# A radix-47 by 64 DFT through DRAM in place of dense DFT matmuls, issued between the MLP steps of the batch ahead

## Chip, cores, metric

One core of one Trainium2 chip. The metric is device time of one execution in microseconds (us); lower is better. A ratio is the mean time of one kernel's fast runs over the mean of the other's fast runs of the same rounds, so it is not quite the ratio of the medians that are quoted beside it. "Batch period" below means the distance between the same point of two successive batches, as a mean of the middle six of one trace: the first matmul of the forward DFT in the kernel before, the first hidden matmul in all other runs.

Engines: PE is TensorE (matmuls), PEld its weight loads, DVE is VectorE, ACT is ScalarE, POOL is GpSimd, SP is SyncE (here only an issuer of DMAs). A "column" is one column of a matmul's moving operand. PSUM holds the tiles that matmuls write here, SBUF those that they read; an "evacuation" is a ScalarE or VectorE copy from PSUM to SBUF. The "pitch" is the time from the start of one matmul to the start of the next, and the "head" is all that comes before the first hidden matmul.

## The reference

A global filter along the sequence, by FFT, followed by an MLP with a "snake" activation:

```
x: [8, 3008, 256]   filt_r, filt_i: [1505, 256]
X = rfft(x, axis=1);  y = irfft(X * (filt_r + 1j*filt_i), n=3008, axis=1)
h = y.reshape(24064, 256) @ w_in           # w_in  [256, 2048]
s = sin(alpha * h)
out = (h + s*s / alpha) @ w_out            # w_out [2048, 256]
```

Both kernels use `out = y @ (w_in @ w_out) + (s*s) @ (w_out / alpha)`. So the MLP has a hidden matmul (y to 2048 features), a Sin on ScalarE, a square on VectorE and a projection.

## The kernel before

The sequence is split into even and odd positions (`r`). Each half is transformed by one dense matmul against cosine and sine tables, combined with the filter on VectorE, and transformed back by another dense matmul. Everything of one batch runs in this order; only the scheduling of independent engines overlaps.

```python
for b in range(B):
    ...                                       # load x, two tiles of 128 x 12 x 256, f16
    for i in range(6):                        # forward DFT
        for p in range(2):                    # cos, sin
            for k in range(12):
                nc.tensor.matmul(out=psA[:, p, :], lhsT=lhs, rhs=xr_tiles[0][0:nrow, k, :], ...)  # 256 columns
                nc.tensor.matmul(out=psB[:, p, :], lhsT=lhs, rhs=xr_tiles[1][0:nrow, k, :], ...)
        nc.scalar.copy(out=asb, in_=psA)
        nc.scalar.copy(out=bsb, in_=psB)
        ...                                   # 28 VectorE operations on 128 x 256: filter and twiddles -> Z
    for r in range(2):
        for cb in range(2):                   # inverse DFT
            for (m0, n) in tok_chunks:        # 512, 512, 480
                for i in range(6):
                    for p in range(2):
                        nc.tensor.matmul(out=psy[:, 0:n], lhsT=Z[r][p][:, i, ...],
                                         rhs=e_t[:, p, i, m0:m0 + n], ...)
                nc.scalar.copy(out=ysb[:, cb, m0:m0 + n], in_=psy[:, 0:n])
        for (m0, n) in tok_chunks:            # MLP
            for jb in range(16):
                ...                           # 2 hidden matmuls of n columns
                nc.scalar.activation(out=vt[:, jb, 0:n], in_=psh[:, 0:n], func=AFT.Sin,
                                     scale=alpha_t[:, jb:jb + 1])
                nc.vector.tensor_tensor(...)  # square
            for t in range(nblk):             # projection: 18 matmuls of 256 columns per 128 tokens
                ...                           # one PSUM buffer; VectorE copy; store to DRAM
```

Of the kernel before, what the change touches and what calls it, by code (L numbers as in the profile page):

```python
# [12 lines left out]
ALU = mybir.AluOpType  # L14


@with_exitstack
def kernel(
# [11 lines left out]
    B, S, C = 8, 3008, 256  # L30
    N = S
    M = S // 2
    NQ = 753
    NQP = 768
    DFF = 2048

    mm = np.arange(M, dtype=np.float64)
    qq = np.arange(NQP, dtype=np.float64)
    qmask = (qq < NQ).astype(np.float64)
    ang = 2.0 * np.pi * np.outer(mm, qq) / M  # L40
    dt_cos = np.cos(ang) * qmask[None, :]
    dt_sin = -np.sin(ang) * qmask[None, :]
    dt_full = np.concatenate([dt_cos, dt_sin], axis=1)
    dt_host = np.zeros((128, 12, 2 * NQP), dtype=np.float16)
    for k in range(12):
        nrow = min(128, M - 128 * k)
        dt_host[:nrow, k, :] = dt_full[128 * k:128 * k + nrow].astype(np.float16)
    e_host = np.zeros((128, 2, 6, M), dtype=np.float16)
    angqm = 2.0 * np.pi * np.outer(qq, mm) / M
    ecos = (np.cos(angqm) * qmask[:, None]).astype(np.float16)  # L50
    esin = (-np.sin(angqm) * qmask[:, None]).astype(np.float16)
    for i in range(6):
        e_host[:, 0, i, :] = ecos[128 * i:128 * (i + 1)]
        e_host[:, 1, i, :] = esin[128 * i:128 * (i + 1)]
    qv = qq.reshape(6, 128).T
    wq = np.where((qv == 0) | (qv == M // 2), 1.0, 2.0) / N
    wq = wq * (qv < NQ)
    wc = wq * np.cos(2 * np.pi * qv / N)
    ws = wq * np.sin(2 * np.pi * qv / N)
    ident_np = np.eye(128, dtype=np.float32)  # L60
    revj_np = np.eye(128, dtype=np.float32)[::-1].copy()

    dt_dram = nc.inline_tensor(dt_host, name="dt_tbl")
    e_dram = nc.inline_tensor(e_host, name="e_tbl")
    w3_dram = nc.inline_tensor(
        np.stack([wq, wc, ws], axis=1).astype(np.float32), name="w3_tbl"
    )
    ident_dram = nc.inline_tensor(ident_np, name="ident")
    revj_dram = nc.inline_tensor(revj_np, name="revj")

    out3 = out.rearrange("(b s) c -> b s c", b=B)

    cpool = ctx.enter_context(tc.tile_pool(name="consts", bufs=1))
    dt_t = cpool.tile([128, 12, 2 * NQP], FP16)
    e_t = cpool.tile([128, 2, 6, M], FP16)
    nc.sync.dma_start(out=dt_t, in_=dt_dram.ap())
    nc.sync.dma_start(out=e_t, in_=e_dram.ap())
    w3_t = cpool.tile([128, 3, 6], FP32)
    nc.sync.dma_start(out=w3_t, in_=w3_dram.ap())
    P0re = cpool.tile([128, 6, C], FP16)  # L80
    P0im = cpool.tile([128, 6, C], FP16)
    Q0re = cpool.tile([128, 6, C], FP16)
    Q0im = cpool.tile([128, 6, C], FP16)
    P1re = cpool.tile([128, 6, C], FP16)
    P1im = cpool.tile([128, 6, C], FP16)
    w_in16 = cpool.tile([128, 2, DFF], FP16)
    nc.gpsimd.dma_start(out=w_in16, in_=moe_w_in.rearrange("(a p) j -> p a j", p=128))
    w_out2 = cpool.tile([128, 16, C], FP16)
    m_t = cpool.tile([128, 2, C], FP16)
    alpha_t = cpool.tile([128, 16], FP32)  # L90
    nc.sync.dma_start(
        out=alpha_t, in_=moe_alpha.rearrange("(a p) -> p a", p=128)
    )
    recip_a = cpool.tile([128, 16], FP32)
    nc.vector.reciprocal(out=recip_a, in_=alpha_t)  # L95

    with tc.tile_pool(name="init", bufs=1) as ipool:
        ident_t = ipool.tile([128, 128], FP32)
        nc.sync.dma_start(out=ident_t, in_=ident_dram.ap())  # L99
        w_in32 = ipool.tile([128, 2, DFF], FP32)  # L100
        nc.sync.dma_start(
            out=w_in32, in_=moe_w_in.rearrange("(a p) j -> p a j", p=128)
        )
        w_out32 = ipool.tile([128, 16, C], FP32)
        nc.sync.dma_start(
            out=w_out32, in_=moe_w_out.rearrange("(b p) c -> p b c", p=128)
        )
        w_out16 = ipool.tile([128, 16, C], FP16)
        w_inT = ipool.tile([128, 16, C], FP16)
        with tc.tile_pool(name="initps", bufs=2, space=bass.MemoryType.PSUM) as ipps:  # L110
            for jb in range(16):
                nc.vector.tensor_scalar(
                    out=w_out2[:, jb, :], in0=w_out32[:, jb, :],
                    scalar1=recip_a[:, jb:jb + 1], scalar2=None, op0=ALU.mult,
                )
                nc.gpsimd.tensor_copy(out=w_out16[:, jb, :], in_=w_out32[:, jb, :])
                for cb in range(2):
                    pst = ipps.tile([128, 128], FP32, tag="pst")
                    nc.tensor.transpose(  # L119
                        out=pst, in_=w_in32[:, cb, jb * 128:(jb + 1) * 128],  # L120
                        identity=ident_t,
                    )
                    nc.vector.tensor_copy(  # L123
                        out=w_inT[:, jb, cb * 128:cb * 128 + 128], in_=pst
                    )
            for cb in range(2):
                psm = ipps.tile([128, 512], FP32, tag="psm")
                for jb in range(16):
                    nc.tensor.matmul(  # L129
                        out=psm[:, 0:C],  # L130
                        lhsT=w_inT[:, jb, cb * 128:cb * 128 + 128],
                        rhs=w_out16[:, jb, :],
                        start=(jb == 0), stop=(jb == 15),
                    )
                nc.vector.tensor_copy(out=m_t[:, cb, :], in_=psm[:, 0:C])
        fr_f = ipool.tile([128, 6, C], FP32)
        fi_f = ipool.tile([128, 6, C], FP32)
        fr_b = ipool.tile([128, 6, C], FP32)
        fi_b = ipool.tile([128, 6, C], FP32)
        nc.sync.dma_start(  # L140
            out=fr_f, in_=filt_r[0:768].rearrange("(i p) c -> p i c", p=128)
        )
        nc.sync.dma_start(
            out=fi_f, in_=filt_i[0:768].rearrange("(i p) c -> p i c", p=128)
        )
        revj_t = ipool.tile([128, 128], FP32)
        nc.sync.dma_start(out=revj_t, in_=revj_dram.ap())
        tfwd = ipool.tile([128, 2, C], FP32)
        with tc.tile_pool(name="revps", bufs=2, space=bass.MemoryType.PSUM) as rpps:
            for i in range(6):  # L150
                row0 = 1377 - 128 * i
                nc.sync.dma_start(out=tfwd[:, 0, :], in_=filt_r[row0:row0 + 128, :])
                nc.sync.dma_start(out=tfwd[:, 1, :], in_=filt_i[row0:row0 + 128, :])
                psrev = rpps.tile([128, 512], FP32, tag="psrev")
                nc.tensor.matmul(out=psrev[:, 0:2 * C], lhsT=revj_t, rhs=tfwd[:, :, :])  # L155
                nc.vector.tensor_copy(out=fr_b[:, i, :], in_=psrev[:, 0:C])
                nc.vector.tensor_copy(out=fi_b[:, i, :], in_=psrev[:, C:2 * C])
        gre = ipool.tile([128, C], FP32)
        gim = ipool.tile([128, C], FP32)
        hre = ipool.tile([128, C], FP32)  # L160
        him = ipool.tile([128, C], FP32)
        ta = ipool.tile([128, C], FP32)
        tb = ipool.tile([128, C], FP32)
        tc_ = ipool.tile([128, C], FP32)
        td = ipool.tile([128, C], FP32)
        for i in range(6):
            wv = w3_t[:, 0, i:i + 1]
            wcv = w3_t[:, 1, i:i + 1]
            wsv = w3_t[:, 2, i:i + 1]
            nc.vector.tensor_tensor(out=gre, in0=fr_f[:, i, :], in1=fr_b[:, i, :], op=ALU.add)  # L170
            nc.vector.tensor_tensor(out=hre, in0=fr_f[:, i, :], in1=fr_b[:, i, :], op=ALU.subtract)
            nc.vector.tensor_tensor(out=gim, in0=fi_f[:, i, :], in1=fi_b[:, i, :], op=ALU.subtract)
            nc.vector.tensor_tensor(out=him, in0=fi_f[:, i, :], in1=fi_b[:, i, :], op=ALU.add)
            if i == 0:
                nc.vector.memset(gim[0:1, :], 0.0)
                nc.vector.memset(him[0:1, :], 0.0)
            nc.vector.tensor_scalar(out=P0re[:, i, :], in0=gre, scalar1=wv, scalar2=None, op0=ALU.mult)
# [19 lines left out]

    tok_chunks = [(0, 512), (512, 512), (1024, 480)]

    for b in range(B):  # L200
        xr_tiles = []
        for r in range(2):
            xt = xpool.tile([128, 12, C], FP16, name=f"x_{b}_{r}", tag=f"x{r}")
# [139 lines left out]
```

## Time and profile before

| | before |
|---|---|
| median of 3 runs | 1392.51 us (1391.48 to 1394.24) |
| first hidden matmul | 156.0 us |
| batch period | 159.4 us |
| TensorE busy in one period | 155.13 us |
| VectorE, ScalarE busy in one period | 88.66, 69.96 us |

The page of the kernel before: busy time per engine, then busy tenths in 40 equal slices of the span ("9" is 90% or more), the granted TensorE clock and the DMA share in the same slices, and the chain of waits that ended last as shares by engine.

```profile
span 1388.4 us, 21372 instructions
PE 1277.2 (92%) x8524; PEld 818.9 (59%) x8524; DVE 752.6 (54%) x2453; ACT 562.1 (40%) x962; POOL 33.2 (2%) x53
...
PE   0629899989999999999999899998999999998998
...
PEclk9859999999999999999999999999999999999999
DMA  9442310030000310121000300103100000000101
...
PE 72%; DVE 21%; SPq 2%; DMA 2%; issue 1%; ACT 1%; POOL 0%; ACTq 0%; DVEq 0%; POOLq 0%
```

TensorE is the limit from the fifth slice on. The head is the exception: the first hidden matmul starts at 156 us.

The table of busy time by stretch of the kernel before: a stretch in us, its length, busy us of each engine with the number of instructions, granted clock, DMA share, GB/s. The stretches are the head and one steady batch.

```profile
core 0: us, PE busy (x) PEld busy (x) DVE busy (x) ACT busy (x) POOL busy (x), PEclk, DMA share, GB/s
0.00:156.00 156.00, 76.86 (x436) 47.66 (x437) 82.14 (x317) 10.91 (x18) 16.88 (x33) 0.85 0.56 145
...
258.10:417.50 159.40, 155.13 (x1059) 100.57 (x1058) 88.66 (x289) 69.96 (x121) 3.27 (x4) 1.00 0.14 30
```

"Busy" must not be read as "at its peak": a matmul's busy span includes time in which the next one already streams. The timeline gives the pitch. Its columns are start, length, engine, line, operation, operands, shapes, count, and in brackets the idle time before it with what ended it. Kernel before, inverse DFT:

```profile
301.29 0.39 PE L261 MATMUL psy_0_0_0_2641<-e_t,z_0_1_2133 128*128 128x512 f16 x1 [2.28 <-DVE z_0_1_2133 L253]
301.51 0.38 PE L261 MATMUL psy_0_0_512_2655<-e_t,z_0_0_2132 128*128 128x512 f16 x1
301.73 0.38 PE L261 MATMUL psy_0_0_512_2655<-e_t,z_0_1_2133 128*128 128x512 f16 x1
```

Each matmul is listed as 0.38 us long, but they start 0.216 us apart: 512 columns in 0.216 us, 2.37 columns per ns. A batch has 352.8 thousand columns, hence 149 of its 159.4 us. The remaining 10 us are waits and paced stretches, such as the 2.28 us on VectorE here.

### The profile page before, as it was taken

The page shows a single profiled execution, that of the slowest core. Times are in us where ns is not written, and L with a number is a line of the kernel's source. Part 1 is how long each engine was busy: PE and PEld are TensorE (multiplying, and loading weights), DVE is VectorE, ACT ScalarE, POOL GpSimd, SP SyncE. Part 2 cuts the span into 40 slices and gives each one's busy share as a digit, 9 for nine tenths or more (in the row PEclk, how much of TensorE's full clock was granted, in tenths as well). Part 3 has the DMA queues.
Part 4 walks back from the last instruction along what each step waited for, and adds up shares of the span by engine and source line. Part 5 has one row for each costly group of instructions (what it writes and reads, how often), then busy time and mean ns, then how long its engine had stood idle before and what let it go on. Part 6 is the DMA issues. An engine that isn't in the chain of part 4 may idle for free.

```text
span 1388.4 us, 21372 instructions
## 1 busy us (share of the span) xinstructions
PE 1277.2 (92%) x8524; PEld 818.9 (59%) x8524; DVE 752.6 (54%) x2453; ACT 562.1 (40%) x962; POOL 33.2 (2%) x53
## 2 busy tenths in 40 slices
PE   0629899989999999999999899998999999998998
PEld 0208465765568465775658565684657655684655
DVE  0757644495256753495355753486444952566534
ACT  0002546316361454416362264414463164613544
POOL 0110000000000000000000000000000000000000
PEclk9859999999999999999999999999999999999999
DMA  9442310030000310121000300103100000000101
GB/s 335 165 66 40 52 38 16 31 45 24 23 31 16 45 35 22 35 35 27 30 24 23 46 31 15 39 10 51 38 16 30 2 23 23 31 15 1 35 19 38
DMA packets 60500, 56.21 MB, mean 40 GB/s; under 512 B 6128, under 2 KB 59632, under 8 KB 59888
## 3 DMA queue, kind: packets, MB, share of 16 engines
q1 hardware_dynamic: 35552, 41.48, 8.6%
q0 software_dynamic: 24848, 13.37, 7.1%
q8 instruction: 66, 1.08, 0.3%
q14 instruction: 34, 0.28, 0.1%
HBM read 43.57 MB, written 24.64 MB: 49 GB/s over the span
## 4 chain that ended last, share of the span: by engine, by line
PE 72%; DVE 21%; SPq 2%; DMA 2%; issue 1%; ACT 1%; POOL 0%; ACTq 0%; DVEq 0%; POOLq 0%
SPq L99 2%; DMA tfwd<-in_filt_i_dram 1%; PE psrev L155 1%; DMA x_1_431<-in_x_dram 1%; PE pst L119 1%; DMA w_in_83<-in_moe_w_in_dram 1%; ACT v_1_1024_13843 L279 0%; PE psm L129 0%; PE psB_0_439 L229 0%; PE psy_0_0_1024_12857 L261 0%; DVE w_inT L123 0%; PE psA_0_7230 L226 0%; PE psA_0_12324 L226 0%; PE psA_0_8928 L226 0%; PE psA_0_3834 L226 0%
## 5 line engine op out<-in xcount | busy, mean ns | idle before, releaser
L273 PEld LDWEIGHTS <-w_in_70 128*128 128x128 f16 x1536 | 149.3, 97 | 101.0 <-issue 19.9
L226 PEld LDWEIGHTS <-dt_t 128*128 128x128 f16 (+1 forms) x1152 | 113.0, 98 | 35.9 <-issue 21.6
L229 PEld LDWEIGHTS <-dt_t 128*128 128x128 f16 (+1 forms) x1152 | 113.5, 99 | 15.7 <-issue 1.4
L119 PE MATMUL pst<-ident_t,w_in_83 128*128 128x128 f32 x32 | 10.6, 402 | 39.7 <-DMA w_in_83<-in_moe_w_in_dram 37.9
L234 ACT ACT_TABLE_LOAD x1 | 1.3, 1283 | 110.1 <-PE psA_0_438 L226 110.1
L119 PEld LDWEIGHTS pst<-ident_t,w_in_83 128*128 128x128 f32 x32 | 5.3, 168 | 44.9 <-issue 37.8
L226 PE MATMUL psA_0_438<-x_0_428,dt_t 128*128 128x256 f16 (+1 forms) x24 | 6.5, 379 | 20.1 <-DMA x_0_428<-in_x_dram 20.1
L155 PE MATMUL psrev<-tfwd,revj_t 128*128 128x512 f32 x12 | 10.4, 963 | 14.2 <-DMA tfwd<-in_filt_i_dram 13.6
L95 DVE RECIPROCAL recip_a<-alpha_t 128x16 f32<-128x16 f32 x1 | 0.3, 255 | 31.2 <-DMA alpha_t<-in_moe_alpha_dram 31.2
L283 DVE TENSOR_TENSOR v_1_0_6713<-v_1_0_6713 128x512 f16<-128x512 f16 x16 | 6.8, 426 | 15.7 <-ACT v_1_0_6713 L279 15.7
L283 DVE TENSOR_TENSOR v_1_0_1619<-v_1_0_1619 128x512 f16<-128x512 f16 x16 | 6.8, 425 | 15.7 <-ACT v_1_0_1619 L279 15.7
L283 DVE TENSOR_TENSOR v_1_0_10109<-v_1_0_10109 128x512 f16<-128x512 f16 x16 | 6.8, 425 | 15.7 <-ACT v_1_0_10109 L279 15.7
L283 DVE TENSOR_TENSOR v_1_0_13505<-v_1_0_13505 128x512 f16<-128x512 f16 x16 | 6.8, 425 | 15.7 <-ACT v_1_0_13505 L279 15.7
L283 DVE TENSOR_TENSOR v_1_0_3317<-v_1_0_3317 128x512 f16<-128x512 f16 x16 | 6.8, 425 | 15.7 <-ACT v_1_0_3317 L279 15.7
L283 DVE TENSOR_TENSOR v_1_0_5015<-v_1_0_5015 128x512 f16<-128x512 f16 x16 | 6.8, 425 | 15.7 <-ACT v_1_0_5015 L279 15.7
L283 DVE TENSOR_TENSOR v_1_0_8411<-v_1_0_8411 128x512 f16<-128x512 f16 x16 | 6.8, 425 | 15.7 <-ACT v_1_0_8411 L279 15.7
L283 DVE TENSOR_TENSOR v_1_0_11807<-v_1_0_11807 128x512 f16<-128x512 f16 x16 | 6.8, 425 | 15.7 <-ACT v_1_0_11807 L279 15.7
L155 PEld LDWEIGHTS psrev<-tfwd,revj_t 128*128 128x128 f32 x12 | 2.6, 269 | 20.6 <-issue 16.1
L123 DVE CAST w_inT<-pst 128x128 f16<-128x128 f32 x32 | 8.4, 290 | 10.2 <-PE pst L119 10.1
L283 DVE TENSOR_TENSOR v_0_0_12913<-v_0_0_12913 128x512 f16<-128x512 f16 x16 | 6.8, 426 | 10.7 <-ACT v_0_0_12913 L279 10.6
L283 DVE TENSOR_TENSOR v_0_0_1027<-v_0_0_1027 128x512 f16<-128x512 f16 x16 | 6.8, 426 | 10.3 <-ACT v_0_0_1027 L279 10.1
L283 DVE TENSOR_TENSOR v_0_0_9517<-v_0_0_9517 128x512 f16<-128x512 f16 x16 | 6.8, 425 | 8.9 <-ACT v_0_0_9517 L279 8.9
(3457 smaller groups left out, 3845.5 us busy)
## 6 DMA issues: line engine op xcount, KB each, us to landing
dt_t<-dt_tbl SPq DMA_DIRECT2D x1, 4608.0 KB, 15.6
e_t<-e_tbl SPq DMA_DIRECT2D x1, 4512.0 KB, 28.7
w_in_83<-in_moe_w_in_dram SPq DMA_DIRECT2D x1, 2048.0 KB, 7.6
w_out_85<-in_moe_w_out_dram SPq DMA_DIRECT2D x1, 2048.0 KB, 13.1
w_in_70<-in_moe_w_in_dram POOLq DMA_DIRECT2D x1, 1024.0 KB, 29.0
fr_f<-in_filt_r_dram SPq DMA_DIRECT2D x1, 768.0 KB, 14.9
fi_f<-in_filt_i_dram SPq DMA_DIRECT2D x1, 768.0 KB, 10.6
tfwd<-in_filt_r_dram SPq DMA_DIRECT2D x6, 128.0 KB, 2.0
```

The lines of the kernel that those rows point to most:

```text
L95: nc.vector.reciprocal(out=recip_a, in_=alpha_t)
L99: nc.sync.dma_start(out=ident_t, in_=ident_dram.ap())
L119: nc.tensor.transpose(out=pst, in_=w_in32[:, cb, jb * 128:(jb + 1) * 128], identity=ident_t,)
L123: nc.vector.tensor_copy(out=w_inT[:, jb, cb * 128:cb * 128 + 128], in_=pst)
L155: nc.tensor.matmul(out=psrev[:, 0:2 * C], lhsT=revj_t, rhs=tfwd[:, :, :])
L226: nc.tensor.matmul(out=psA[:, p, :], lhsT=lhs, rhs=xr_tiles[0][0:nrow, k, :], start=(k == 0), stop=(k == 11))
L229: nc.tensor.matmul(out=psB[:, p, :], lhsT=lhs, rhs=xr_tiles[1][0:nrow, k, :], start=(k == 0), stop=(k == 11))
L234: nc.scalar.copy(out=asb, in_=psA)
L273: nc.tensor.matmul(out=psh[:, 0:n], lhsT=w_in16[:, cb, jb * 128:jb * 128 + 128], rhs=ysb[:, cb, m0:m0 + n], start=(cb == 0), stop=(cb == 1),)
L283: nc.vector.tensor_tensor(out=vt[:, jb, 0:n], in0=vt[:, jb, 0:n], in1=vt[:, jb, 0:n], op=ALU.mult,)
```

## The change

The intent is to cut TensorE columns. 3008 = 47 x 64, so the DFT is done in two small stages forward (47 points, then 64 with the twiddle factors folded into the tables) and two back. Between stages the data must change which axis lies on the partitions; that is done by writing to DRAM and reading back in another order (`d1`, `d2`). The pieces of batch b+1's DFT are issued between the 48 MLP steps of batch b. Along with this come: hidden matmuls into PSUM tiles of 2 x 512 columns with one Sin over all 1024, alpha folded into w_in, chunks that run across batch borders (so that all have multiples of 128 tokens), and two projection PSUM buffers. The diff, cut to its core:

```diff
-            for k in range(12): ...            # 288 forward matmuls x 256 columns a batch
-                nc.tensor.matmul(out=psy[:, 0:n], lhsT=Z..., rhs=e_t[...])   # 144 inverse x 480..512
+    def spectral(b, y_new, off):
+        def stage1(u):                          # 8 pieces, 2 matmuls each: K=94, M=96, 512 columns
+            ...
+                nc.tensor.matmul(out=ps[0:NK, :], lhsT=wf_t, rhs=st["x"][ch][:, n0:n0 + 2, :], ...)
+                evac(st["t1"][:, n0:n0 + 2, :], ps[0:NK, :])      # alternates ScalarE / VectorE
+            if half == 1:
+                nc.sync.dma_start(out=d1_rows[...], in_=st["t1"])
+            if u == 7: ...                      # read d1 back as t2, 8 DMAs
+        def stage2(u):                          # 13 pieces
+            ...                                 # 2 matmuls with d_t (256 columns), ScalarE copy -> xf
+            ...                                 # 2 VectorE products with the filter
+            ...                                 # 4 matmuls with e_t (256 columns), evac -> g, write d2
+        def stage3(u):                          # 16 pieces, 4 matmuls each: K=96, M=128, 94 columns
+            if rest == 0: ...                   # read d2 back as t4
+            psv = ps....rearrange("p (a r) -> p a r", r=NR)
+            for i in range(4):
+                nc.tensor.matmul(out=psv[:, i, :], lhsT=st["t4"][...], rhs=wi_t, ...)
+            dst = y_new[:, cb, off:off + S].rearrange("p (r n) -> p n r", n=32)[:, n0:n0 + 4, :]
+            evac(dst, psv)
...
+    starts = {1: 0, 2: 13, 3: 31}               # MLP step (of 48) at which a stage begins
+    steps = {1: 8, 2: 16, 3: 16}                # over how many steps it is spread
+        for j in range(8):
+            hidden(k, j)                        # 4 matmuls, Sin over 2 x n, square
+            while pending and pending[0][0] <= step:
+                pending.pop(0)[1]()             # a piece of the next batch's DFT
+            ...                                 # half projections of chunk k-1
+            step += 1
```

In the code above, `t1`, `t2`, `t4` appear in profiles as `t`, `d1` and `d2` as `d`; `pa`, `pb`, `pc`, `pd` are the PSUM tiles of stage 1, stage 2 forward, stage 2 inverse and stage 3; `ph` and `po` those of hidden and projection; `w` is w1 or w2 or their float32 source tiles by number.

## The prediction

> **What bounds it now.** The chain of waits is 72% TensorE. In the table of busy time by stretch every steady 160 us holds 155 to 157 us of TensorE, against 89 of VectorE and 70 of ScalarE. The tile records show one batch every 159.4 us (second batch's forward DFT from 258.1, third's from about 417). The first MLP matmul starts at 156 us: that prologue is constants (9 MB of DFT tables ahead of the weights), the filter combination and an un-overlapped first DFT.
>
> Pitches from the timeline: 16 projection matmuls (256 columns) issue 0.109 us apart, 12 inverse-DFT matmuls (512 columns) take 2.59 us, 0.216 each, so about 2.37 columns per ns. Columns per batch: forward DFT 288x256 = 73.7k, inverse 72.2k, hidden 96.3k, projection 110.6k; sum 352.8k, 149 us at pitch. 10 of 159 us are stalls (waits for z on VectorE, the single projection PSUM buffer, ScalarE-paced hidden steps at 0.57 us).
>
> **What the change does.** DFT columns per batch fall from 145.9k to 16x512 + 72x256 = 26.6k (11.2 us), plus 64 stage-3 matmuls of 94 columns. Those are bound by weight loads: 0.097 us each in the trace; [...] The MLP keeps 204.5k columns, 86.3 us. So TensorE needs about 104 us per batch; with 2.5% stalls 106.5. All of the saving is on the critical path, since TensorE is.
>
> ScalarE: Sin over 1024 columns. From 512 (0.57 us pitch) and 480 (0.543) the slope is 0.84 ns per column, so 1.0 us; 47 of them, 26 copies of 0.585 and 8 smaller: about 66 us. VectorE: 47 squares of 0.70, 24 products of 0.425, evacuations and outputs: about 65 us, well below today's 89. Neither binds.
>
> Moved: relayouts through DRAM, 6 MB more per batch; with input and output 12 MB in 106 us, 115 GB/s, while the first slice shows 335. Stage 1 ends 5 steps (11 us) before stage 2 starts; stage 2 ends 3 steps (6.6 us) before stage 3. I expect 0 to 3 us of waiting at the latter per batch. [...]
>
> Prologue: estimate first hidden matmul at about 105 us: inputs, filters, then w_in and w_out (queued behind the filter copies) by 55; folding and transposes to 68; stage 2 to 88; relayout and stage 3 to 105.
>
> **Sum:** 105 + 7x106.5 + 89 (last batch, no DFT) + 5 = **945 us**, range 905 to 1000. Faster by over 2%: 0.97; within 2%: 0.02; slower: 0.01.
>
> **What would show it.** Batches 104 to 109 us apart; TensorE above 93% busy there at a clock near 0.99; [...] ScalarE and VectorE near 65 us per batch; first hidden matmul 95 to 125 us; no large TensorE wait on DMA after that.
>
> **What would make it wrong.** Relayout DMAs slower than the slack (stalls of 5 to 10 us per batch, 35 to 70 in all); [...] a prologue of 130 us or more; cross-engine waits in the fine interleave above 5%; a lower granted clock.

The cut estimate was part of the "about 104 us" of TensorE per batch; with the 0.097 us that still stand, stage 3 is 64 x 0.097 = 6.2 us and the sum 86.3 + 11.2 + 6.2 = 103.7 us. The loads of 94 rows had no term in the sum.

## The result, and the profile after

| | before | after | predicted |
|---|---|---|---|
| median, same rounds | 1393.38 us (1391.48 to 1394.71) | 941.43 us (939.14 to 947.77) | 945, 905 to 1000 |
| ratio | | 0.6764 (95%: 0.6739 to 0.6788) | |
| first hidden matmul | 156.0 us | 120.9 us | 105 |
| batch period | 159.4 us | 103.3 us (middle six) | 106.5 |
| seven batches with a DFT in them | | 719 us | 745.5 |
| last batch and tail | | 101.1 us | 94 |

The page of the kernel after:

```profile
span 941.0 us, 14994 instructions
PE 836.2 (89%) x6201; PEld 583.6 (62%) x6201; DVE 570.9 (61%) x878; ACT 594.8 (63%) x662; POOL 88.1 (9%) x136
...
PE   3027289999999999999999999999999999999997
...
PEclk9999589999999999999999999999999999999999
DMA  9961254324523083316423281407432242400101
...
PE 47%; issue 25%; DMA 10%; ACT 4%; POOL 2%; DVE 2%; SPq 1%; POOLq 0%; DVEq 0%; ACTq 0%
```

TensorE is still full from the sixth slice on. The chain holds less of it (47%, with 25% "issue"), and DMA has risen from 2% to 10%: the relayouts of the DFTs (the trips through DRAM) now lie in the chain. That share alone does not say that they cost anything; the waits decide that.

The table by stretch of the kernel after, for the head, two batches and the last batch:

```profile
core 0: us, PE busy (x) PEld busy (x) DVE busy (x) ACT busy (x) POOL busy (x), PEclk, DMA share, GB/s
0.00:120.90 120.90, 36.64 (x217) 22.76 (x218) 44.68 (x72) 33.26 (x39) 6.97 (x16) 0.90 0.64 167
...
426.90:530.30 103.40, 101.54 (x760) 70.56 (x758) 69.68 (x106) 73.81 (x83) 10.62 (x16) 1.00 0.40 106
839.90:941.00 101.10, 94.64 (x680) 66.08 (x677) 42.74 (x64) 48.90 (x49) 10.56 (x15) 0.99 0.10 39
```

A steady batch is 98% TensorE at clock 1.00 (97% in the kernel before), but 56 us shorter. ScalarE holds 73.8 us and VectorE 69.7, more than the 65 or so predicted.

The timeline of the kernel after, around two pieces of stage 3 in a steady batch:

```profile
196.41 0.33 PE L207 MATMUL pd_4_1443<-wi_t,t_1_1_1441 96*128 96x94 f16 x4
196.58 1.15 PE L336 MATMUL po_0_1380<-w_192,v_1165 128*128 128x256 f16 x9
197.56 1.03 PE L318 MATMUL ph_4_1461<-y_103,w_191 128*128 128x512 f16 x4
```

Four stage-3 matmuls take 0.17 us, 0.042 each; the prediction had the 0.097 us of a weight load.

The waits of TensorE from 121 to 930 us, kernel after, the longest ones (waited for, us in total, times, longest):

```profile
PE pb_0_848 L168 <- DMA t_1_0_743<-d_1_619: 2.1, 1, 2.1
PE ph_0_623 L318 <- ACT y_103 L126: 1.7, 1, 1.7
PE pb_0_2027 L168 <- DMA t_2_0_1910<-d_2_1737: 1.4, 1, 1.4
PE pd_0_2527 L207 <- DMA t_2_0_2525<-d_2_1738: 1.3, 1, 1.3
```

All waits for relayouts together are about 12 us over seven batches, under 2 a batch. So the DMA share of the chain is nearly all hidden behind the MLP.

The head is less good. Timeline of the kernel after, three moments of it: the issue of w_in, its first use, and one of the first stage-3 evacuations:

```profile
42.55 2.66 SPq L263 DMA_DIRECT2D w_in_205<-in_moe_w_in_dram  x1
...
58.87 4.49 DVE L274 TENSOR_TENSOR w_191<-w_in_205,al_bc 128x2048 f16<-128x2048 f32 x2 [29.96 <-DMA w_in_205<-in_moe_w_in_dram]
61.22 0.61 PE L283 MATMUL pst_0_234<-id_197,w_191 128*128 128x128 f16 x4 [32.53 <-DVE w_191 L274]
...
104.44 1.88 ACT L126 CAST y_103<-pd_2_528 128x376 f16<-128x376 f32 x1 [0.56 <-PE pd_2_528 L207]
```

TensorE waits 32.5 us for the weights; stage 1 is done by then, but stage 2 stands behind the weight preparation in program order. And the stage-3 evacuation of 376 columns takes 1.88 us, where the prediction's ScalarE sum leaves about 0.47 us for it (66 us less 47 and 26 x 0.585, over 8 copies); a 128x512 copy of ScalarE in the same trace takes 0.59 us (`w1T`).

### The profile page after: what moved, and what is told of

It reads as the page before. It is cut to its first block, busy times and chain, and to the rows that moved or that the text cites. A ratio compares the mean times of both kernels' runs of the same rounds, so it can differ in the third digit from the quotient of the medians.

```text
span 941.0 us, 14994 instructions
## 1 busy us (share of the span) xinstructions
PE 836.2 (89%) x6201; PEld 583.6 (62%) x6201; DVE 570.9 (61%) x878; ACT 594.8 (63%) x662; POOL 88.1 (9%) x136
## 4 chain that ended last, share of the span: by engine, by line
PE 47%; issue 25%; DMA 10%; ACT 4%; POOL 2%; DVE 2%; SPq 1%; POOLq 0%; DVEq 0%; ACTq 0%
POOL out_dram L344 2%; ACT y_103 L126 2%; DMA d_2_1737<-t_2_3_1879 1%; DMA d_6_6491<-t_6_3_6633 1%; DMA d_5_5293<-t_5_3_5455 1%; DMA d_4_4114<-t_4_3_4256 1%; DMA d_1_619<-t_1_3_722 1%; DMA t_3_0_3723<-d_3_2917 0%; DMA t_1_0_1346<-d_1_620 0%; DMA t_5_0_6100<-d_5_5294 0%; DMA t_2_0_2525<-d_2_1738 0%; DMA d_2_1738<-g_9_2411 0%; SPq L194 0%; DMA d_4_4115<-g_9_4788 0%; PE po_0_6530 L336 0%
## 5 line engine op out<-in xcount | busy, mean ns | idle before, releaser
L318 PEld LDWEIGHTS <-w_191 128*128 128x128 f16 x1536 | 150.2, 98 | 100.1 <-issue 1.4
L187 PEld LDWEIGHTS <-e_t 128*128 128x128 f16 x384 | 37.3, 97 | 14.9 <-issue 6.3
L148 PEld LDWEIGHTS <-wf_t 94*96 94x96 f16 x128 | 16.6, 130 | 34.8 <-issue 20.8
L168 PEld LDWEIGHTS <-d_t 128*128 128x128 f16 x192 | 18.3, 98 | 29.5 <-DMA t_1_0_743<-d_1_619 2.6
L283 PE MATMUL pst_0_234<-id_197,w_191 128*128 128x128 f16 x4 | 0.6, 306 | 32.5 <-DVE w_191 L274 32.5
L283 PEld LDWEIGHTS <-w_191 128*128 128x128 f16 x32 | 3.2, 137 | 36.2 <-DVE w_191 L274 34.5
L274 DVE TENSOR_TENSOR w_191<-w_in_205,al_bc 128x2048 f16<-128x2048 f32 x2 | 4.5, 2288 | 30.0 <-DMA w_in_205<-in_moe_w_in_dram 30.0
L322 DVE TENSOR_TENSOR v_4311<-v_4311 128x1024 f16<-128x1024 f16 x8 | 5.5, 692 | 9.1 <-ACT v_4311 L321 9.1
L322 DVE TENSOR_TENSOR v_6688<-v_6688 128x1024 f16<-128x1024 f16 x8 | 5.5, 693 | 9.1 <-ACT v_6688 L321 9.1
L322 DVE TENSOR_TENSOR v_1934<-v_1934 128x1024 f16<-128x1024 f16 x8 | 5.5, 692 | 9.1 <-ACT v_1934 L321 9.1
L322 DVE TENSOR_TENSOR v_5509<-v_5509 128x1024 f16<-128x1024 f16 x8 | 5.5, 693 | 8.8 <-ACT v_5509 L321 8.8
L322 DVE TENSOR_TENSOR v_8986<-v_8986 128x1024 f16<-128x1024 f16 x8 | 5.5, 693 | 8.3 <-ACT v_8986 L321 8.3
L322 DVE TENSOR_TENSOR v_755<-v_755 128x1024 f16<-128x1024 f16 x8 | 5.5, 692 | 8.2 <-ACT v_755 L321 8.2
L322 DVE TENSOR_TENSOR v_9123<-v_9123 128x1024 f16<-128x1024 f16 x8 | 5.5, 693 | 8.0 <-ACT v_9123 L321 8.0
L322 DVE TENSOR_TENSOR v_9260<-v_9260 128x1024 f16<-128x1024 f16 x8 | 5.5, 693 | 8.0 <-ACT v_9260 L321 8.0
L322 DVE TENSOR_TENSOR v_9397<-v_9397 128x1024 f16<-128x1024 f16 x8 | 5.5, 693 | 8.0 <-ACT v_9397 L321 8.0
L322 DVE TENSOR_TENSOR v_9534<-v_9534 128x1024 f16<-128x1024 f16 x8 | 5.5, 693 | 8.0 <-ACT v_9534 L321 8.0
L322 DVE TENSOR_TENSOR v_3132<-v_3132 128x1024 f16<-128x1024 f16 x8 | 5.5, 693 | 8.0 <-ACT v_3132 L321 8.0
L322 DVE TENSOR_TENSOR v_7886<-v_7886 128x1024 f16<-128x1024 f16 x8 | 5.5, 692 | 8.0 <-ACT v_7886 L321 8.0
## 6 DMA issues: line engine op xcount, KB each, us to landing
filt_101<-in_filt_r_dram POOLq DMA_DIRECT2D x2, 384.0 KB, 17.6
```

The costliest lines, as they stand in the source:

```text
L148: nc.tensor.matmul(out=ps[0:NK, :], lhsT=wf_t, rhs=st["x"][ch][:, n0:n0 + 2, :], start=True, stop=True)
L168: nc.tensor.matmul(out=ps[:, i, :], lhsT=d_t[:, s, :], rhs=st["t2"][s // 6][:, s % 6, :], start=True, stop=True)
L187: nc.tensor.matmul(out=ps[:, i, :], lhsT=e_t[:, k, 2 * w + i, :], rhs=pr[k][:, i, :], start=(k == 0), stop=(k == 1))
L274: nc.vector.tensor_tensor(out=w1[:, cb, :], in0=w_in32[:, cb, :], in1=al_bc, op=ALU.mult)
L283: nc.tensor.transpose(out=pst[:, i, :], in_=w1[:, cb, jb * 128:jb * 128 + 128], identity=id16)
L318: nc.tensor.matmul(out=ps[:, i, 0:n], lhsT=w1[:, cb, jb * 128:jb * 128 + 128], rhs=y[b][:, cb, t0:t0 + n], start=(cb == 0), stop=(cb == 1))
```

## The experiments

The theory after the result: (A) the gain is the TensorE columns, collected because the small pieces run between MLP steps; (B) the prediction's two errors are a stage 3 that costs TensorE less than thought and a head that costs more, and the head is longer because of the strided evacuation and of the order of the loads. The rivals: the gain comes from the other parts of the change (larger PSUM tiles, fewer VectorE operations, shorter head), or the relayouts still hold the batch back.

### pad_columns: put the removed columns back

```diff
+    def pad(b, ps, n):
+        if b > 0:
+            for _ in range(n):
+                nc.tensor.matmul(out=ps, lhsT=d_t[:, 0, :], rhs=e_t[:, 0, 0:4, :], start=True, stop=True)
...
                 ps = fps.tile([128, 512], FP32, name=f"pa_{b}_{u}_{i}", tag="f")
+                pad(b, ps, 3)
...              # 6 before each stage-2 inverse tile (12 for the last), 6 before each stage-3 tile
```

The 222 extra matmuls of 512 columns in each batch after the first write tiles that are then overwritten; the result stays right, and the column count is within 1% of the kernel before.

> The changed kernel with 222 extra 512-column matmuls per later batch (results overwritten), spread over the 37 DFT pieces, so that TensorE again streams as many columns per batch as the dense kernel; interleave, relayouts and prologue untouched. Theory A (the gain is the columns taken off TensorE, the binding engine): 113.7k columns at 2.37 per ns are 48 us per batch, 7 batches 335 us, so 941 becomes 1260 to 1280, batches 150 to 152 us apart. Theory B (the gain is the interleave filling TensorE's gaps, so that TensorE now has room): most of the extra matmuls fit into gaps and the time stays under 1100.

Measured: 1263.92 us (1262.6 to 1265.3), ratio to before 0.9073. Period 149.8 us. Table by stretch of this run:

```profile
280.00:430.00 150.00, 149.95 (x994) 93.78 (x993) 72.61 (x108) 76.47 (x82) 11.37 (x17) 1.00 0.28 74
```

As theory A expected. The period rises by 46.5 us, against 222 x 0.216 = 48 us of added matmul time. So in this schedule columns are worth 322 of the 452 us gained. At the old column count the new kernel still has a period 10 us shorter (149.8 against 159.4): that is the worth of the interleaving and of the other parts together, which no run separates. Between the profiled executions of the kernel before and of this run (1388.4 and 1263.5 us), the seven periods from first hidden to first hidden matmul differ by 77 us (1119.1 against 1042.3), the head by 36 and the stretch after the first hidden matmul of the last batch by 12 (113.3 against 101.1): in the kernel before, half of the inverse DFT still lies in that stretch.

### mlp_only: leave the later DFTs out (wrong on purpose)

```diff
+    nc.vector.memset(y[0][:, :, S:S + 64], 0.0)
...
             if b + 1 < B:
-                y[b + 1] = new_y(b + 1)
...              # the loop over spectral(b + 1, ...) goes
+                y[b + 1] = y[0]
```

> Wrong result on purpose: the DFT of batches 1 to 7 is left out, all MLP steps read batch 0. Theory A: what a DFT costs in the steady state is its own TensorE time plus its waits, so 376 MLP steps of 1.85 us after the 121 us prologue and 5 us of tail give 815 to 830 us; 941 minus this, over 7, is 16 to 18 us per DFT. Theory B (the DFT hides in gaps of the MLP): 900 us or more.

Measured: 818.48 us (817.66 to 819.4); the result is wrong, as meant. By the expectation's own sum a DFT costs (941.4 - 818.5) / 7 = 17.6 us a batch, but this counts a shorter head too: without the second batch's input loads the first hidden matmul comes at 112.86 us, 8.1 earlier, and TensorE waits 25.3 us for the weights in place of 32.5. The period is 86.8 us:

```profile
194.90:281.60 86.70, 86.70 (x609) 59.36 (x608) 40.04 (x60) 48.75 (x49) 8.53 (x12) 1.00 0.09 36
```

So a DFT costs 103.3 - 86.8 = 16.6 us of a steady batch. Its matmuls take 26.6 thousand columns, 11.2 us, and 64 x 0.042 = 2.7 us for stage 3: 13.9 us. The other 2.7 us go to waits, the relayouts' among them.

### block_end: the same DFT, not interleaved

```diff
-                    pending.append((starts[stage] + i * steps[stage] / count[stage], piece))
+                    pending.append((47, piece))
```

All pieces of the next batch's DFT are issued at the last MLP step of the current one.

> The same work with no interleave: all pieces of the next batch's DFT are put at the last step of the batch ahead; the order of instructions shows stages 2 and 3 alone on TensorE there. Theory A with interleave as its condition: stages 2 and 3 alone take what they take in the prologue (17.5 and 19.5 us, with 7.5 us of relayout between, and some 8 us of relayout after stage 1), so about 30 to 36 us more per batch and 1150 to 1200 us. If the interleave were only a detail: under 1000.

Measured: 1278.05 us (1276.4 to 1280.1), ratio 0.9178, some 80 us above the expected range: the direction was right, and the loss larger than thought. Period 151.1 us. Waits of TensorE from 120 to 1250 us in this run, then one batch by stretch:

```profile
PE pd L207 <- ACT y L126: 79.9, 49, 1.7
PE pb L168 <- DMA t<-d: 57.5, 7, 9.6
PE pd L207 <- DMA t<-d: 57.3, 7, 9.0
PE pc L187 <- ACT xf L171: 25.1, 35, 0.7
```

```profile
210.80:362.00 151.20, 113.70 (x770) 75.76 (x768) 73.72 (x108) 77.92 (x82) 11.14 (x17) 0.86 0.26 75
```

Of the 47 us by which this stretch is longer than the 104.40 us one of the kernel after (219.90 to 324.30, where TensorE was busy for 101.52), 34.6 us are more idle time (37.5 against 2.9), and 12.2 us are more busy time for nearly the same number of matmul records (770 and 760), at a granted clock of 0.86 in place of 1.00. The idle time is what was expected (30 to 36 us); the lower clock is what the expectation left out. The run has relayout waits of up to 9.6 us; that such idle times brought the clock down is the author's reading, and no run tests it.

The same reduction in columns is worth 115 us of 1393 when it is not interleaved, and 452 when it is. Not all of the loss is relayouts, though: of the idle time in the stretch above, 17.3 us are waits for them and 12.9 us waits for stage 3's slow evacuation (see below). With the evacuation of evac_read4 one block may lose less; no run shows it.

### slack_less: shorter distance between stages

```diff
-    starts = {1: 0, 2: 13, 3: 31}
+    starts = {1: 0, 2: 9, 3: 26}
```

> Stages 2 and 3 are asked for earlier (steps 9 and 26 for 13 and 31). If the relayout latency is just covered by the slack in the changed kernel (its TensorE waits for t2 and t4 add up to about 2 us per batch), taking 4 steps and 1 step away brings 4 to 11 us of waiting per batch: 970 to 1020. If the slack has room to spare: 945 or less.

Measured: 975.77 us (970.1 to 978.4), at the low end of what was expected. The seven waits for the first relayout are now 22.6 us, up to 4.6 each, and the period 107.7 us. So the distances in the kernel after are near the least that hides the relayouts.

### slack_more: longer distance

```diff
-    starts = {1: 0, 2: 13, 3: 31}
-    steps = {1: 8, 2: 16, 3: 16}
+    starts = {1: 0, 2: 15, 3: 34}
+    steps = {1: 8, 2: 15, 3: 13}
```

> Stages 2 and 3 are asked for later (steps 15 and 34 for 13 and 31). The waits for t2 and t4 in the changed kernel add up to about 13 us over 7 batches; if they are all that is left of the relayouts on the critical path, this gives 926 to 934. If other stalls hide behind them: 938 to 943.

Measured: 941.71 us (941.26 to 941.75), ratio 0.6763 against the kernel's 0.6764: nothing gained, as its second theory had it. Waits of TensorE from 121 to 930 us in this run:

```profile
PE ph L318 <- DVE y L128: 5.0, 7, 0.7
PE pd L207 <- ACT y L126: 4.4, 7, 0.7
PE pd L207 <- DVE y L128: 1.4, 4, 0.3
PE pb L168 <- DMA t<-d: 0.2, 1, 0.2
```

The waits for DMA are gone, as intended, but waits for the evacuation of stage 3 (`y`) took their place: stage 3 now has 13 steps in place of 16, and each evacuation holds its engine for almost 2 us (1.81 to 1.87 us in a steady batch of the kernel after). Waits for DMA alone were not the cost; the slow evacuation was the next in line.

### evac_run4 and evac_read4: two ways to write y in runs of four tokens

The evacuation writes y with 94 elements of 2 bytes, 64 bytes apart, for each of 4 positions. The four positions are neighbours in y, so turning the order around writes runs of 8 bytes. In evac_run4 the matmul writes PSUM with a stride, so that the evacuation reads it in order:

```diff
-            psv = ps....rearrange("p (a r) -> p a r", r=NR)
+            psv = ps....rearrange("p (r a) -> p r a", a=4)
-                nc.tensor.matmul(out=psv[:, i, :],
+                nc.tensor.matmul(out=psv[:, :, i],
-            dst = y_new[...].rearrange("p (r n) -> p n r", n=32)[:, n0:n0 + 4, :]
+            dst = y_new[...].rearrange("p (r n) -> p r n", n=32)[:, :, n0:n0 + 4]
```

> Stage 3's matmuls write PSUM interleaved, so that each evacuation writes runs of 4 adjacent tokens to y instead of single 2-byte elements 64 bytes apart; same elements, same count. If the 1.88 us of a 128x376 evacuation (a contiguous 128x512 takes 0.585) comes from the stride of its writes: 0.45 to 0.7 us each, stage 3 of the prologue 7 to 9 us instead of 19.5, the first hidden matmul near 110, total 926 to 932; the later batches stay near 103 us because TensorE sets them. If it comes from reading PSUM or from something else: 1.9 us and 941 again.

Measured: 950.83 us (949.1 to 952.6), ratio 0.683: slower than the kernel after and outside the expected range, though the first hidden matmul came at 112.25 us. The timeline of evac_run4 shows why:

```profile
190.85 0.49 PE L207 MATMUL pd<-wi_t,t 96*128 96x94 f16 x4
191.13 1.19 PE L336 MATMUL po<-w,v 128*128 128x256 f16 x9
```

Four matmuls now take 0.28 us in place of 0.17, that is 64 x 0.028 = 1.8 us a batch more of TensorE, the engine that binds; the period rose to 105.2. The evacuation fell to 0.47 us on ScalarE and 0.55 on VectorE. So the theory of the slow evacuation stood, and this cure moved its price to the matmul; the next run was made to tell these apart.

In evac_read4 the matmul writes PSUM in order and the evacuation reads with the stride:

```diff
-            dst = y_new[...].rearrange("p (r n) -> p n r", n=32)[:, n0:n0 + 4, :]
-            evac(dst, psv)
+            dst = y_new[...].rearrange("p (r n) -> p r n", n=32)[:, :, n0:n0 + 4]
+            evac(dst, psv.rearrange("p a r -> p r a"))
```

> As evac_run4, but the matmuls write PSUM contiguously again and the evacuation reads PSUM with the stride. evac_run4 cut the evacuation to 0.47 to 0.55 us and still lost, with stage-3 matmuls 0.070 us apart instead of 0.042. If the stride of the matmul's PSUM writes was the loss: matmuls back to 0.042, evacuations 0.47 to 0.7 us, batches 103 us, total 927 to 934. If the reordered evacuation itself costs the batches: 945 to 951 again.

Measured: 926.34 us (925.88 to 927.55), ratio 0.6653, just below the expected range. First hidden matmul at 108.83 us, 12.1 us earlier; period 102.7; stage-3 matmuls again 0.042 us apart. The groups of instructions of evac_read4 (busy us, mean ns of one, idle before it):

```profile
L128 DVE CAST y<-pd 128x376 f16<-128x376 f32 x64 | 35.0, 547 | 32.2 <-PE pd L207 32.2
L126 ACT CAST y<-pd 128x376 f16<-128x376 f32 x64 | 29.9, 468 | 14.8 <-PE pd L207 14.7
```

Both are as fast as in evac_run4 (550 and 468 ns), so reading PSUM with this stride costs the two engines nothing measurable. The three kernels together (after, evac_run4, evac_read4): the evacuation's time goes with the order of its SBUF writes (1.88 us for single elements 64 bytes apart, 0.47 to 0.55 for runs of 8 bytes), the matmul's with the order of its PSUM writes (0.042 us in order, 0.070 with the stride).

### early_weights: load the weights first

```diff
-        nc.sync.dma_start(out=w_in32, ...)
+        nc.scalar.dma_start(out=w_in32, ...)    # likewise w_out32 and al_bc: ScalarE's queue, from the start
```

> w_in, w_out and the broadcast alpha are loaded from the ScalarE queue at the start instead of behind the relayout reads and the filter copies on SyncE. If the prologue overran because TensorE waited 32 us for w_in (landed at 58.9): stage 2 starts at 50 to 56 instead of 76.5, total 915 to 922. If the DMA engines, which are full for the first 60 us, set the prologue: the other loads are pushed back and the gain is under 8 us, 933 to 941.

Measured: 934.7 us (934.3 to 944.9). The first hidden matmul came 11.7 us earlier (109.23), but the total fell by 6.7 only, within the second theory's range: the DMA engines are full in the first 60 us in both orders (share 1.04 and 1.05). The ratios, 0.6738 (0.6699 to 0.6777) and 0.6764 (0.6739 to 0.6788), overlap, so the total is not clearly better. In this run TensorE waits 16.5 us for x, and stage 1 stretches to about 37 us. Between the profiled executions the total fell by 8.6 us: about 3 us of the gain were given back in the seven batches (721.9 us in place of 719.0), most of it in the first.

### combo: early weights, evac_run4 and stage 2 ahead of the weights

```diff
+    for _, piece in first[8:21]:                # stage 2 of batch 0, before the weight preparation
+        piece()
...              # and the edits of early_weights and evac_run4
```

> early_weights, evac_run4, and stage 2 of the first batch ahead of the weight folding on TensorE. If the prologue terms add: first hidden matmul at 80 to 92 us, total 898 to 912, batches unchanged. If the first 60 us are set by the DMA engines: 920 to 928, no better than evac_run4 by more than 8.

Measured: 940.3 us (936.5 to 941.8): missed both ranges. The head was shorter (104.2 us), but the first table of stage 1 came late (TensorE waited 16.6 us), and the period was near 105 us as in evac_run4, whose strided PSUM write was still in it: 21.1 us of waits for the first relayout came on top.

### prologue: stage 2 of the first batch ahead of the weight preparation

```diff
+            if b == 1:                          # batch 1's x loads wait until w1 is made
+                nc.gpsimd.tensor_copy(out=xt[0:1, 0, 0:2], in_=st_t["w1"][0:1, 0, 0:2])
...
+    for _, piece in first[8:21]:
+        piece()
...
-            nc.vector.tensor_tensor(out=w1[:, cb, :], in0=w_in32[:, cb, :], in1=al_bc, op=ALU.mult)
+            nc.gpsimd.tensor_tensor(out=w1[:, cb, :], in0=w_in32[:, cb, :], in1=al_bc, op=ALU.mult)
```

> First batch's stage 2 ahead of the weight folding on TensorE, the folding multiply on GpSimd, and the second batch's input load held back until the weights are folded; the weight loads stay where they are. If the prologue is set by what has to cross the DMA engines before stage 2 (about 13 MB instead of 18 at 266 GB/s): stage 2 starts at 48 to 56, first hidden matmul at 88 to 102, total 907 to 924. If it is set by something else: 935 or more.

Measured: 927.35 us (925.8 to 931.7), ratio 0.6662; the first hidden matmul came at 104.51 us, 16.4 earlier; period 103.3, unchanged. A few us short of what was expected. The run makes three edits at once and does not separate them; mlp_only, which has no second batch to load, bounds one: there the head is 8.1 us shorter.

### best: prologue, evac_read4 and a little more slack

The edits of prologue and evac_read4, and

```diff
-    starts = {1: 0, 2: 13, 3: 31}
-    steps = {1: 8, 2: 16, 3: 16}
+    starts = {1: 0, 2: 14, 3: 32}
+    steps = {1: 8, 2: 15, 3: 15}
```

> prologue and evac_read4 together with slightly later stages 2 and 3 (steps 14 and 32). If their gains add: first hidden matmul at 80 to 94, batches 102 to 103, total 893 to 912. If not: no better than prologue alone.

Measured: 907.73 us (906.24 to 910.67), ratio 0.6519, as expected. First hidden matmul at 94.76 us, period 102.2. So 26.1 us of the gain over the kernel after lie in the head and 8.1 us in the seven batches (710.9 in place of 719.0). Timeline of best, VectorE and GpSimd:

```profile
49.73 0.76 DVE L179 TENSOR_TENSOR p<-xf,filt 128x512 f16<-128x512 f16 x2 [0.40 <-ACT xf L175]
51.52 9.18 DVE L179 TENSOR_TENSOR p<-xf,filt 128x512 f16<-128x512 f16 x2 [1.03 <-ACT xf L175]
...
51.30 9.12 POOL L282 TENSOR_TENSOR w<-w_in,al_bc 128x2048 f16<-128x2048 f32 x2 [45.33 <-DMA w_in<-in_moe_w_in_dram]
```

While the GpSimd multiply ran, two VectorE products took 9.18 us in place of 0.76: each (4.55 and 4.71 us) started just after one of the two GpSimd multiplies (4.49 and 4.66 us) and ended just after it.

### best2: the multiply back on VectorE, after the products

```diff
+            nc.vector.tensor_copy(out=w1[0:1, cb, 0:2], in_=st_t["xf"][0:1, 0, 0:2])   # not before the last xf
-            nc.gpsimd.tensor_tensor(out=w1[:, cb, :], ...)
+            nc.vector.tensor_tensor(out=w1[:, cb, :], ...)
```

> The best version, but the multiply that folds alpha into w1 goes back from GpSimd to VectorE and is held until the products of stage 2 of the first batch are done. In the best version two of those products took 9.18 us in all, against 0.76 us otherwise, while the GpSimd multiply ran (9.12 us). Theory 1: that sharing was the loss; then the products take 0.4 us each throughout, stage 2 ends some 9 us sooner, the first hidden matmul starts at 84 to 90 us in place of 94.8, and the total is 896 to 904 us. Theory 2: the wait for the filter's copies, hence the DMA, sets the prologue anyway; the first hidden matmul stays above 92 us and the total at 905 to 910 us.

Measured: 907.88 us (904.84 to 908.73), ratio 0.6512: equal to best. The products were freed, and the first hidden matmul came at 89.78 us, 5.0 earlier, in theory 1's range; the total, where theory 1 expected 896 to 904, did not move and lies in theory 2's range. So each theory had half of it. The timeline of best2 shows the products at full speed, and where the 5 us were given back:

```profile
51.70 0.76 DVE L180 TENSOR_TENSOR p<-xf,filt 128x512 f16<-128x512 f16 x2 [1.05 <-ACT xf L175]
...
117.86 0.55 PE L172 MATMUL pb<-t,d_t 128*128 128x256 f16 x2 [2.15 <-DMA t<-d]
```

Stage 2 of the second batch waits 2.15 us for its relayout (0.16 in best). By stretch, best2:

```profile
110.00:114.00 4.00, 4.00 (x30) 2.83 (x29) 2.08 (x4) 2.16 (x3) 0.76 (x1) 1.00 0.06 16
...
115.70:117.86 2.16, 0.01 (x2) 0.01 (x1) 0.69 (x1) 1.02 (x1) 0.00 (x0) 1.00 1.09 263
117.86:120.00 2.14, 2.14 (x11) 1.52 (x12) 0.76 (x2) 0.59 (x1) 0.00 (x0) 0.52 1.18 242
120.00:122.00 2.00, 2.00 (x10) 0.96 (x9) 0.00 (x0) 0.20 (x1) 0.00 (x0) 0.66 0.82 171
122.00:124.00 2.00, 2.00 (x17) 1.41 (x16) 1.14 (x2) 1.18 (x2) 0.00 (x0) 1.00 0.00 0
```

After that wait the clock is 0.52 and then 0.66; an estimate from these figures is 2.14 x 0.48 + 2.00 x 0.34 = 1.7 us more. With a longer wait before stage 3 (1.15 against 0.56 us) this makes 4.3 us, and the first batch takes 4.2 us longer than in best (102.0 against 97.9 us). In the kernel after, a wait of 2.10 us (before 145.61) was followed by a clock of 1.00, so what brought it down here is not shown. Why this relayout took some 2 us longer than in best stays open. Most of it arose before its reads were issued (at 112.91 us, 7.7 us after stage 1's last write was issued, against 6.0 in best), and from 110 to 114 us the DMA engines were nearly idle (0.06); their share of about 1.1 as the wait ends is the relayout's own reading. All this is from the profile of one run, and no run tests it.

Best and best2 differ in the engine of the multiply and in its start, held back in best2 to 63.95 us, and the same two products took 9.18 us beside the GpSimd multiply and 0.76 without it: the slowing was real, and it was not what set the total.

## Why the prediction was right

**The mechanism: right.** Most of the gain is TensorE columns on the critical path. pad_columns gives back 322 of the 452 us with columns alone, and a steady batch is 98% TensorE at clock 1.00 (predicted: above 93%, 0.99).

**The batch period: right in kind, 3 us too long.** Predicted 106.5, measured 103.3, so its stated test, 104 to 109, was missed by a little. The mis-sized term is stage 3: 6.2 us from the 0.097 us of a weight load, measured 64 x 0.042 = 2.7 us. The other terms stand: 86.3 + 11.2 + 2.7 = 100.2 us, and 3.1 us of waits (3%, predicted 2.5%). Each of these matmuls has a weight load of its own, of 97 ns, and still four of them issue in 0.17 us: 94 columns in 0.042 us are 2.24 columns per ns, near the 2.37 of the 512-column matmuls. The busy length of a weight load was no lower bound on the pitch of these four.

**Relayout waits: right in size.** Predicted 0 to 3 us a batch before stage 3, measured 0.8 there on average. The waits before stage 2, for which the prediction allowed nothing with its 11 us of slack, are as large (6.7 us in all); together they stay under 2 a batch. That they depend on the slack is shown by slack_less (22.6 us of waits for the first relayout in seven batches). The x loads of 94 rows did not hold the batches back: those of the later batches landed in 5 to 8 us, for 376 KB each as the trace counts them. From 125.5 to 131 us the packets of two of these loads took 55 us in all, within 5.0 us, the time of some 11 of the 16 engines; the trace does not name the engines.

**VectorE and ScalarE: too low, without effect on the total.** Predicted about 65 and 66 us, measured 69.7 and 73.8. The wrong term is the stage-3 evacuation, 1.88 us against about 0.47: with the fast one of evac_read4 a steady batch holds 60.7 us of VectorE and 64.2 of ScalarE. It did not bind in a steady batch, but held back slack_more.

**The head: the step that failed most.** "First hidden matmul at about 105 us", measured 120.9. By its own steps: w_in by 55 (58.9), folding to 68 (76.5), stage 2 to 88 (93.6), relayout and stage 3 to 105 (120.9). The last step, 17 us predicted and 27.3 measured, makes up 10.3 of the 15.9 us, and it is the strided evacuation: without it (evac_read4) the head is 12.1 us shorter. Of the rest, 3.9 us are w_in, which stands behind the filter copies in the queue, on DMA engines that are full up to 60 us (share 1.02 to 34 us, then 1.06), and 4.6 us the folding (17.6 us in place of 13): its 32 matmuls of 256 columns took 6.4 us, 0.20 each, where a steady batch has 0.109. Stage 2 was 2.9 us shorter than predicted.

**The last batch: a forgotten term.** "89 (last batch, no DFT) + 5", measured 101.1: the projection of the last chunk, 7.85 us, runs after the last hidden step and was not counted.

The errors are +15.9 (head), -26.5 (seven batches; one part of this is the first of them, 99.0 us, which has no projection of an earlier chunk to do) and +7.1 (end): together -3.5 us. The total is therefore closer than its terms were; part of the agreement is luck.

## What to carry to other kernels

Removing work from the binding engine pays in full only if the small dependent pieces that replace it can be issued between other work of that engine: here the same DFT was worth 115 us in one block and 452 interleaved, with enough steps between its stages to hide each relayout. For an evacuation that also permutes, look at the run length on the SBUF side (here 1.88 us against 0.47 to 0.55), and try the stride on the engine's PSUM read (here no measurable cost) rather than on the matmul's PSUM write (here 0.070 us a matmul against 0.042). When a head is shortened, look for the next point at which the binding engine waits: 5 us won at the first matmul were given back, from 28 us later on.
